# A mixture of experts whose first layer changes from twelve products a tile to Strassen's seven, in two long jobs an expert

## The chip, the cores and the metric

One core of a Trainium2 chip runs the whole program: attention and, behind and beside it, a mixture of experts. The metric is the device time of one execution in microseconds; a comparison is of medians over executions. Engines are named as in the profile: PE (TensorE, matmuls), PEld (its weight loads), DVE (VectorE), ACT (ScalarE), POOL (GpSimd, which also issues the indirect transfers) and SP (SyncE, which issues the plain ones). Each engine takes its instructions in the order in which the program holds them.

## The reference

`q`, `k`, `v` are 8 batches x 8 heads x 576 places x 64. Four heads attend to the 32 places before, four to places of the same remainder by 32. The result, 4608 rows of 512, goes through a mixture of eight experts, two of them for each row:

```python
logits = x @ w_gate
noisy_logits = logits + np.log1p(np.exp(x @ w_noise)) * noise
top2 = np.argpartition(-noisy_logits, 2, axis=1)[:, :2]
# top2_w: softmax over the two
for e in range(8):
    for k in range(2):
        mask = top2[:, k] == e
        h = np.maximum(x[mask] @ w1[e], 0.0)          # 512 -> 1024
        out[mask] += top2_w[mask, k, None] * (h @ w2[e])   # 1024 -> 512
```

All is float32. Which rows an expert gets is known only on the chip.

## The kernel before, in words

Attention runs first, with the gate and, for each expert, a list in memory of the rows (tokens) that chose it and their weights. An expert's list has 1216 places here: nine blocks of 128, and a half block of 64 that is empty for some experts.

**Matmuls of three products.** A float32 operand is split in a high and a low part of the type that TensorE takes at full rate; a product is hi x hi + lo x hi + hi x lo, three matmuls. The high part is a cast by ACT, the low part a subtraction by DVE: of the weights in `weights_of` (L905, L906), of the gathered rows in `transposes` (L1029, L1031), of the hidden layer in `layer1` (L1080, L1085).

**Jobs.** A job is an expert and a stretch of its list, (start, blocks, tail, batches that must be done). Before, experts 3 to 7 have four jobs each: three blocks from place 256, two from 640, two and the half block from 896, two from 0. Experts 0 to 2 have some of theirs early, beside attention. For each job the loop at the end of `experts` puts down: the gather of the next job's rows (POOL, four transfers a block, L982, into `xg`, two deep), layer 1, the loads and splits of the next expert's weights, the next job's transposes (DVE, L1022) and splits, and layer 2.

**Layer 1** (`layer1`, L1060) has eight tiles of 128 hidden features; each is one PSUM bank with 4 x 3 matmuls of the job's width, 256 or 384 columns, or 320 with a tail. In a job with a tail the ten inner matmuls run at 320, 288 or 256 columns by a value read on the chip. ACT's Relu gives the high part from the bank, DVE the low part.

**Layer 2** (`layer2`, L1114) has a bank a block: 24 matmuls of 512 columns; for the half block 16, or one of zeros (L1123) where it is empty. ACT scales the bank by the rows' weights into `prev` (L1138; for a half block DVE adds the second half, L1142), and POOL scatters `prev` to the result rows with an adding transfer (L1147).

**The order.** All this is put down as `Piece`s (engine, cost, what they read, write and allocate). `issue_all` walks them like a simulation: of the pieces whose predecessors are placed it places next, for each engine, the one that by its costs could start first, by rank where several could within 120 ns. A cost is 60 + 0.84 ns a column for ACT, 75 + 1.04 for DVE; a PSUM bank is handed to the piece that asks, free since longest first. `Ring` is a tile name with its depth: the k-th next allocation waits for the users of the one k before. POOL's transfers get a wait on the DVE or ACT instruction that the planner put ahead of them. So the costs and the rings, not the text, fix the order on each engine.

## Time and profile before

| | us |
|---|---|
| median of 3 executions | 1124.09 |
| lowest, highest | 1120.41, 1124.75 |
| the profiled execution, its own time | 1126.48 |
| its span in the trace | 1124.7 |
| mean granted clock of TensorE | 0.979 |

The page sums busy time of each engine over the span, shows it in 40 slices, and follows the chain of work that ended last back from the end. Rows of the chain and of the timeline give the start, the length and what ran; rows of groups give the busy sum, the mean in ns and the idle time before. Busy time of PE is a union of overlapping matmuls, so the length of one matmul row is longer than the distance to the next.

### The profile page before, as it was taken

To read this page: it belongs to the slowest core of one execution; us is meant where nothing else is said; L and a number is where in the kernel's file an instruction comes from. 1 tells how busy PE (TensorE), PEld (TensorE's weight loads), DVE (VectorE), ACT (ScalarE), POOL (GpSimd) and SP (SyncE) were. 2 spreads that over 40 slices of the span, in tenths; PEclk is the share of its full clock that TensorE was granted. 3 is DMA by queue.
4 is the path that set the end of the run, shared out by engine and by line. 5 is a ranking of instruction groups with operands and counts; after the bars stand their busy time and mean duration, and the time that the engine had idled before them with its cause. 6 is when DMAs were issued, how large, how long until landed. Compare 5 with 4: busy or idle time off the path is not lost.

```text
span 1124.7 us, 23405 instructions
## 1 busy us (share of the span) xinstructions
PE 1076.4 (96%) x8729; PEld 949.0 (84%) x8729; DVE 551.6 (49%) x1532; ACT 483.9 (43%) x1205; POOL 530.5 (47%) x654
## 2 busy tenths in 40 slices
PE   9888898998999999999999999999999999999994
PEld 7667677887889988998899989898989898898993
...
GB/s 187 183 167 212 209 168 202 203 191 215 231 78 156 114 49 44 125 119 120 123 130 131 46 63 184 54 46 81 167 46 48 109 130 43 56 149 54 43 33 22
DMA packets 167946, 133.01 MB, mean 118 GB/s; under 512 B 51636, under 2 KB 136116, under 8 KB 167812
## 3 DMA queue, kind: packets, MB, share of 16 engines
...
q14 instruction: 52, 0.43, 0.1%
HBM read 92.84 MB, written 39.39 MB: 118 GB/s over the span
## 4 chain that ended last, share of the span: by engine, by line
PE 86%; DVE 4%; issue 3%; ACT 3%; DMA 2%; another core or an unknown queue 1%; POOL 0%; POOLq 0%; DVEq 0%; ACTq 0%
PE bankH L1114 5%; PE bankD L1114 5%; PE bankE L1060 5%; PE bankB L1060 5%; PE bankA L1060 5%; PE bankC L1060 5%; PE bankH L1060 4%; PE bankB L1114 4%; PE bankF L1060 4%; PE bankG L1060 4%; PE bankD L1060 4%; PE bankA L1114 4%; PE bankF L1114 4%; PE bankC L1114 4%; PE bankE L1114 4%; PE bankG L1114 4%
## 5 line engine op out<-in xcount | busy, mean ns | idle before, releaser
L982 POOL DMA_INDIRECT xg<-x_dram,gxx x240 | 245.8, 1024 | 183.0 <-DVE xr L1022 80.7
L1147 POOL DMA_INDIRECT out_dram<-prev,tabt x80 | 135.3, 1691 | 104.2 <-ACT prev L1138 64.8
L833 POOL DMA_INDIRECT tab<-ent,addr x96 | 93.2, 971 | 106.6 <-issue 27.3
L1022 DVE STREAM_TRANSPOSE xr<-xg 128x512 f32<-128x512 f32 (+1 forms) x64 | 66.5, 1039 | 42.4 <-DMA xg<-x_dram,gxx 33.1
L1029 ACT CAST xhi<-xr 128x512 fp32r<-128x512 f32 (+1 forms) x64 | 37.8, 591 | 61.2 <-DVE xr L1022 58.9
L906 DVE TENSOR_TENSOR w2lo<-wraw,w2hi 128x512 fp32r<-128x512 f32 x80 | 52.2, 684 | 13.5 <-ACT w2hi L905 7.5
L906 DVE TENSOR_TENSOR w1lo<-wraw,w1hi 128x512 fp32r<-128x512 f32 x80 | 54.6, 686 | 2.8 <-issue 0.4
L1031 DVE TENSOR_TENSOR xlo<-xr,xhi 128x512 fp32r<-128x512 f32 (+1 forms) x64 | 42.2, 659 | 27.2 <-ACT xhi L1029 25.7
L905 ACT CAST w1hi<-wraw 128x512 fp32r<-128x512 f32 x80 | 49.0, 616 | 3.4 <-issue 3.3
L905 ACT CAST w2hi<-wraw 128x512 fp32r<-128x512 f32 x80 | 46.7, 618 | 7.4 <-DMA wraw<-in_moe_w_dram 6.4
L821 POOL COPY ent<-wt 96x12 f32<-96x12 f32 x8 | 1.6, 201 | 93.2 <-DVE wt L815 82.8
L1085 DVE SCALAR_TENSOR_TENSOR hlo<-bankE,hhi 128x256 fp32r<-128x256 f32 (+1 forms) x33 | 15.2, 460 | 58.1 <-ACT hhi L1080 39.8
L1060 PE MATMUL bankB<-xhi,w1hi 128*128 128x256 f32 (+3 forms) x136 | 40.8, 300 | 0.0
L1060 PE MATMUL bankE<-xhi,w1hi 128*128 128x256 f32 (+3 forms) x132 | 40.5, 307 | 0.0
L1060 PE MATMUL bankB<-xhi,w1lo 128*128 128x256 f32 (+3 forms) x136 | 40.3, 296 | 0.0
L1060 PE MATMUL bankB<-xlo,w1hi 128*128 128x256 f32 (+3 forms) x136 | 40.2, 295 | 0.0
L1060 PE MATMUL bankE<-xhi,w1lo 128*128 128x256 f32 (+3 forms) x132 | 40.0, 303 | 0.0
L1060 PE MATMUL bankE<-xlo,w1hi 128*128 128x256 f32 (+3 forms) x132 | 39.8, 302 | 0.0
L1060 PE MATMUL bankA<-xhi,w1hi 128*128 128x256 f32 (+3 forms) x128 | 38.9, 304 | 0.0
L1085 DVE SCALAR_TENSOR_TENSOR hlo<-bankD,hhi 128x256 fp32r<-128x256 f32 (+1 forms) x31 | 14.2, 458 | 50.0 <-ACT hhi L1080 40.0
L1060 PE MATMUL bankH<-xhi,w1hi 128*128 128x256 f32 (+3 forms) x128 | 38.6, 302 | 0.0
L1060 PE MATMUL bankC<-xhi,w1hi 128*128 128x256 f32 (+3 forms) x128 | 38.4, 300 | 0.0
...
## 6 DMA issues: line engine op xcount, KB each, us to landing
...
```

What stands on the lines that cost most here:

```text
L821: nc.gpsimd.tensor_copy(s["ent"].t[:, :, :, 1].bitcast(F32), s["wt"].t)
L833: st = nc.gpsimd.indirect_dma_start(out=tab, out_offset=bass.IndirectOffsetOnAxis(ap=s["addr"].t[:, t, kk:kk + 1], axis=0), in_=s["ent"].t ...
L905: Piece("ACT", act(512) + 30, lambda o: nc.scalar.copy(hi.t, raw.t), rank, read=[raw], alloc=[hi], expert=True)
L906: Piece("DVE", dve(512), lambda o: nc.vector.tensor_tensor(lo.t, raw.t, hi.t.bitcast(F32), ALU.subtract), rank, read=[raw, hi], alloc=[lo] ...
L982: dma(lambda o, g=g: nc.gpsimd.indirect_dma_start(out=xg.t[:, g, :], out_offset=None, in_=x_dram[:4 * known, :], in_offset=bass.IndirectOf ...
L1022: Piece("DVE", 8 * rows, lambda o, xg=xg, xr=xr, ng=ng, rows=rows: nc.vector.transpose(xr.t.rearrange("p (c x) -> p c x", c=ND)[:, :, :row ...
L1029: Piece("ACT", act(4 * rows), lambda o, view=view, cols=cols: nc.scalar.copy(xh.t[:, :, cols], view()), rank, read=[xr], expert=True, **{h ...
L1031: Piece("DVE", dve(4 * rows), lambda o, view=view, cols=cols: nc.vector.tensor_tensor(xl.t[:, :, cols], view(), xh.t[:, :, cols].bitcast(F ...
L1060: nc.tensor.matmul(ps.t[:, :width], a.t[:, 128 * d:128 * d + 128], c.t[:, d, :width], start=(m == 0), stop=(m == len(todo) - 1))
L1085: nc.vector.scalar_tensor_tensor(dst, ps.t[:, c0:c1], 0.0, hh.t[:, c0:c1].bitcast(F32), op0=ALU.max, op1=ALU.subtract)
L1114: nc.tensor.matmul(ps.t, HT[n, f][p[0]].t[:, cols], W2[n][f][p[1]].t, start=(m == 0), stop=(m == len(todo) - 1))
L1147: st = nc.gpsimd.indirect_dma_start(out=out[:known, :], out_offset=bass.IndirectOffsetOnAxis(ap=tb.t[:rows, i, 0:1], axis=0), in_=pv.t[:ro ...
```

## The change

Experts 3 to 7 get two jobs each, four blocks and the half from place 640 (576 places) and five blocks from 0 (640 places); the last part of expert 1 becomes one job of 576. Layer 1 of these eleven jobs is computed by Strassen's scheme with 7 products in Winograd's form: the rows are cut into two halves of 288 or 320 columns, the 512 inputs into two halves of 256, the 1024 features into pairs of tiles (i, i + 4). For each of four pairs `pair` makes seven products of 2 x 3 matmuls. They use seven combinations of weights (three quarters of `wraw` as loaded, and four sums in `Sa` and `Sb`, made by four adds of 256 columns on POOL) and seven of inputs (`XR` as transposed, and four sums `TS` on DVE), each split in hi and lo. Three banks a pair (a, b, f) take the products; ACT copies the first to `CC` (two deep), DVE combines the others with `CC`, ACT and DVE make the hi and lo parts `hp`. `ends` copies the half block's columns to a spare place. The half block's 64 places are always computed in layer 1. Layer 2 reads `hp` and has the same matmuls.

The new tiles take the place in SBUF of old ones: a `GATE` piece closes a pool when its last users are placed and opens the new one in its place. `prev` has three tiles instead of four. In the last job, the result rows of the job's places are gathered ahead (`previous`, POOL), DVE adds bank times weight to them, and the scatter writes without adding. A setting of the program's indirect transfers, `dynamic_dma_scratch_size`, becomes 8192.

```diff
-        [(0, 2, 0, 4), (256, 3, 0, 5), (640, 2, 0, B), (896, 2, 64, B)],
+        [(0, 2, 0, 4), (256, 3, 0, 5), (640, 4, 64, B)],
         [(0, 3, 0, 7), (384, 2, 0, 7), (640, 2, 0, 7), (896, 2, 64, B)],
-    ] + [[(0, 2, 0, B), (256, 3, 0, B), (640, 2, 0, B), (896, 2, 64, B)]] * (E - EARLY)
+    ] + [[(0, 5, 0, B), (640, 4, 64, B)]] * (E - EARLY)
     WID = 384
+    FAST = 4
+    HALF = 320
...
+    def swap(old, new, users, side):
+        def change(o):
+            if old:
+                spaces[old].close()
+            open_pool(new, side)
+        gates_at[new] = Piece("GATE", 0, change, 0, after=users)
...
-            ("prev", [128, DM], F32, 4)):
+            ("tabt", [128, 5, 3], I32, 3), ("gix", [128, 5], I32, 3), ("tabx", [128, 20, 3], I32, 2),
+            ("gxx", [128, 5, 4], I32, 2), ("xg", [128, 4, 128], F32, 2), ("prev", [128, DM], F32, 3)):
         R[name] = ring(ffn, shape, dtype, name, depth)
-    for layer in (1, 2):
-        for part in ("hi", "lo"):
-            R[f"w{layer}{part}"] = ring(wring, [128, 512], F32R, f"w{layer}{part}", NF)
+    for name, shape, dtype, depth in (
+            ("xr", [128, ND * 128], F32, 1), ("xhi", [128, ND, WID], F32R, 1), ("xlo", [128, ND, WID], F32R, 1),
+            ("w1hi", [128, 512], F32R, NF), ("w1lo", [128, 512], F32R, NF)):
+        R[name] = ring(pools["wplain"], shape, dtype, name, depth)
+    for name in ("hhi", "hlo"):
+        R[name] = ring(pools["hplain"], [128, WID], F32R, name, NF)
+    for part in ("hi", "lo"):
+        R[f"w2{part}"] = ring(wring, [128, 512], F32R, f"w2{part}", NF)
+    NPR = NF // 2
+    for where, name, shape, dtype, depth in (
+            ("xfast", "XR", [128, ND, 2 * HALF], F32, 1), ("xfast", "TS", [128, 4, HALF], F32, 1),
+            ("xfast", "xBhi", [128, 3, 2, HALF], F32R, 1), ("xfast", "xBlo", [128, 3, 2, HALF], F32R, 1),
+            ("xfast", "xThi", [128, 4, 2, HALF], F32R, 1), ("xfast", "xTlo", [128, 4, 2, HALF], F32R, 1),
+            ("xfast", "Sa", [128, 2, 256], F32, 1), ("xfast", "Sb", [128, 2, 256], F32, 1),
+            ("xfast", "CC", [128, 3 * HALF], F32, 2),
+            ("wfast", "fhi", [128, 7, 256], F32R, NPR), ("wfast", "flo", [128, 7, 256], F32R, NPR),
+            ("hfast", "hp", [128, 2, 4 * HALF], F32R, NPR)):
...
+        def add(dst, x, y):
+            nc.gpsimd.tensor_tensor(dst, x, y, ALU.add)
+        def first(o):
+            add(sa.t[:, 0, :], rb.t[:, :256], rb.t[:, 256:])
+            add(sa.t[:, 1, :], sa.t[:, 0, :], ra.t[:, :256])
+        def second(o):
+            add(sb.t[:, 0, :], ra.t[:, :256], rb.t[:, :256])
+            add(sb.t[:, 1, :], ra.t[:, 256:], sa.t[:, 1, :])
+        Piece("POOL", 1300, first, rank, read=[ra, rb], alloc=[sa], expert=True)
+        Piece("POOL", 1300, second, rank, read=[ra, rb, sa], alloc=[sb], expert=True)
...
+        parts = ((ra, lambda: ra.t.rearrange("p (a x) -> p a x", a=2), 0, 2), (rb, lambda: rb.t[:, None, 256:], 2, 3),
+                 (sa, lambda: sa.t, 3, 5), (sb, lambda: sb.t, 5, 7))
+        for src, view, a, b in parts:
...
+            split(bh, bl, lambda t: t[:, 0, :, :w], lambda: xr.t[:, :2, :w], [xr], "alloc", 2 * w)
+            for kk in range(2):
+                ts = R["TS"].new()
+                def sums(o, kk=kk, ts=ts):
+                    b11, b12 = xr.t[:, kk, :w], xr.t[:, kk, w:2 * w]
+                    b21, b22 = xr.t[:, 2 + kk, :w], xr.t[:, 2 + kk, w:2 * w]
+                    t = [ts.t[:, i, :w] for i in range(4)]
+                    nc.vector.tensor_tensor(t[0], b11, b12, ALU.subtract)
+                    nc.vector.tensor_tensor(t[1], t[0], b22, ALU.add)
+                    nc.vector.tensor_tensor(t[2], b12, b22, ALU.subtract)
+                    nc.vector.tensor_tensor(t[3], b21, t[1], ALU.subtract)
...
+            product(a, 0, bh, bl, 0, True, False, psum=[a, b, f])
+            x = step("ACT", act(w) + 30, lambda o: nc.scalar.copy(c21(), bank(a)()), read=[a], alloc=[cc])
+            product(b, 4, th, tl, 1, True, False, write=[b])
+            u2 = step("DVE", dve(w), tt(c12, c21, bank(b), ALU.subtract), read=[b, cc], write=[cc])
+            product(f, 3, th, tl, 0, True, False, write=[f])
+            w_ = step("DVE", dve(w), tt(c22, c21, bank(f), ALU.add), read=[f, cc], write=[cc])
+            product(a, 1, bh, bl, 1, False, True, write=[a], after=[x])
+            step("ACT", act(w) + 30, lambda o: nc.scalar.activation(hp.t[:, 0, :w], bank(a)(), AF.Relu), read=[a], alloc=[hp])
+            product(b, 5, th, tl, 2, False, False, write=[b], after=[u2])
+            v = step("DVE", dve(w), tt(c22, bank(b), c22, ALU.subtract), read=[b, cc], write=[cc])
+            def low(dst, src, hi):
+                nc.vector.scalar_tensor_tensor(dst, src, 0.0, hi.bitcast(F32), op0=ALU.max, op1=ALU.subtract)
+            product(f, 6, bh, bl, 2, False, True, write=[f], after=[w_])
+            step("DVE", dve(w), tt(c12, c12, bank(f), ALU.add), read=[f, cc], write=[cc])
+            step("DVE", dve(w), lambda o: low(hp.t[:, 1, :w], bank(a)(), hp.t[:, 0, :w]), read=[a, hp], write=[hp])
+            product(b, 2, th, tl, 3, False, True, write=[b], after=[v])
+            step("DVE", dve(w), tt(c21, bank(b), c21, ALU.subtract), read=[b, cc], write=[cc])
+            step("ACT", act(3 * w) + 30, lambda o: nc.scalar.activation(hp.t[:, 0, w:4 * w], cc.t[:, :3 * w], AF.Relu),
+                 read=[cc], write=[hp])
+            step("DVE", dve(3 * w), lambda o: low(hp.t[:, 1, w:4 * w], cc.t[:, :3 * w], hp.t[:, 0, w:4 * w]), read=[cc, hp],
+                 write=[hp])
+            if jobs[n][1][2]:
+                def ends(o):
+                    spare = hp.t[:, :, 4 * HALF - 128:].rearrange("p s (a g x) -> p a s g x", a=2, g=2)
+                    for part in range(2):
+                        nc.scalar.copy(spare[:, part], hp.t[:, part, :4 * w].rearrange(
+                            "p (s g x) -> p s g x", s=2, g=2)[:, :, :, w - 32:].bitcast(F32))
+                step("ACT", 2 * act(128), ends, read=[hp], write=[hp])
...
+        def previous(n, i, rank, others):
+            gi = G_[n][1]
+            if n + 1 < NJOB:
+                return None
+            pv = R["prev"].new()
+            dma(lambda o: nc.gpsimd.indirect_dma_start(
+                out=pv.t, out_offset=None, in_=out,
+                in_offset=bass.IndirectOffsetOnAxis(ap=gi.t[:, i:i + 1], axis=0)),
+                128 * 2048, rank, eng="POOL", read=[gi], alloc=[pv], after=others + zero, expert=True)
+            return pv
...
+            if kept:
+                Piece("DVE", dve(512), lambda o: nc.vector.scalar_tensor_tensor(
+                    pv.t, ps.t, tb.t[:, i, 1:2].bitcast(F32), pv.t, op0=ALU.mult, op1=ALU.add), rank, expert=True,
+                      read=[ps, tb, pv], write=[pv])
...
-                    **({} if first else {"compute_op": ALU.add}))
+                    **({} if first or kept else {"compute_op": ALU.add}))
...
+            if turned:
+                swap("wplain", "wfast", users_of("w1hi", "w1lo", "xhi", "xlo", "xr") + [gates_at["xfast"]], "right")
```

Three places of the instruction order, as they stand in the programs (the operation, the tile written and those read, its shape, and on what it waits: an engine's name is that engine, DMAHW and DMASW a transfer).

On PE, the start of a job of 384 columns of an expert, before:

```order
L1060 MATMUL bankC<-xhi,w1hi 128x384 [waits Activation_49]
L1060 MATMUL bankC<-xlo,w1hi 128x384 [waits DVE_49]
L1060 MATMUL bankC<-xhi,w1lo 128x384
L1060 MATMUL bankC<-xhi,w1hi 128x384
...
L1060 MATMUL bankD<-xhi,w1hi 128x384
L1060 MATMUL bankD<-xlo,w1hi 128x384
```

and of the change, in the first two pairs of a job of 640 places:

```order
L1188 MATMUL bankF<-xBhi,fhi 128x320
...
L1188 MATMUL bankD<-xBhi,fhi 128x320 [waits Activation_49]
...
L1188 MATMUL bankC<-xThi,fhi 128x320
...
L1188 MATMUL bankE<-xThi,fhi 128x320
...
L1188 MATMUL bankG<-xThi,fhi 128x320 [waits Activation_49]
...
L1188 MATMUL bankF<-xBhi,fhi 128x320 [waits Activation_49]
...
L1188 MATMUL bankC<-xThi,fhi 128x320 [waits DVE_49]
...
L1188 MATMUL bankE<-xBhi,fhi 128x320 [waits DVE_49]
```

Before, a job goes on from bank to bank without a wait once its inputs are there; now two pairs stand interleaved, and a bank is used again within the pair after ACT or DVE has read it.

On DVE, between the bank readers of a job of 384 before:

```order
L1085 SCALAR_TENSOR_TENSOR hlo<-bankC,hhi 128x384 [waits Activation_49]
L906 TENSOR_TENSOR w2lo<-wraw,w2hi 128x512 [waits DMAHW2_49,Activation_49]
L906 TENSOR_TENSOR w2lo<-wraw,w2hi 128x512 [waits DMAHW3_49,Activation_49]
L1085 SCALAR_TENSOR_TENSOR hlo<-bankD,hhi 128x384 [waits Activation_49]
L906 TENSOR_TENSOR w2lo<-wraw,w2hi 128x512 [waits DMAHW4_49,Activation_49]
L1085 SCALAR_TENSOR_TENSOR hlo<-bankF,hhi 128x384 [waits Activation_49]
```

and of the change, in a job of 640 places:

```order
L1196 TENSOR_TENSOR CC<-bankG,CC 128x320 [waits PE_49]
L989 TENSOR_TENSOR flo<-wraw,fhi 128x512 [waits DMAHW4_49,Activation_49]
L989 TENSOR_TENSOR flo<-wraw,fhi 128x256 [waits DMAHW5_49,Activation_49]
L1212 SCALAR_TENSOR_TENSOR hp<-CC,hp 128x960 [waits Activation_49] x2
L1196 TENSOR_TENSOR CC<-CC,bankB 128x320 [waits PE_49,Activation_49]
L989 TENSOR_TENSOR flo<-Sa,fhi 128x512 [waits Pool_49]
L1196 TENSOR_TENSOR CC<-CC,bankD 128x320 [waits PE_49]
L989 TENSOR_TENSOR flo<-Sb,fhi 128x512 [waits Pool_49]
```

The next expert's weight low parts, some of which wait for POOL's sums, now stand between combinations that PE waits for.

On DVE, behind the last low parts of expert 0, before:

```order
L1085 SCALAR_TENSOR_TENSOR hhi<-bankG,hhi 128x64
L1031 TENSOR_TENSOR xlo<-xr,xhi 128x4x128 [waits Activation_49]
L906 TENSOR_TENSOR w1lo<-wraw,w1hi 128x512 [waits DMAHW3_49,PE_49,Activation_49]
L1022 STREAM_TRANSPOSE xr<-xg 128x4x4x32 [waits DMASW3_49,DMASW2_49,DMASW5_49,DMASW0_49,DVE_49]
L1031 TENSOR_TENSOR xlo<-xr,xhi 128x4x128 [waits Activation_49]
```

and the end of what stands there ahead of the first new products' inputs:

```order
L1149 TENSOR_TENSOR xTlo<-TS,xThi 128x4x288 [waits Activation_49]
L989 TENSOR_TENSOR flo<-Sa,fhi 128x512 [waits Pool_49]
L1159 TENSOR_TENSOR TS<-XR 128x288 [waits DVE_49]
L1160 TENSOR_TENSOR TS<-TS,XR 128x288 [waits DVE_49]
L1161 TENSOR_TENSOR TS<-XR 128x288
L1162 TENSOR_TENSOR TS<-XR,TS 128x288 [waits DVE_49]
L1362 SCALAR_TENSOR_TENSOR prev<-bankC,tabt,prev 64x512 [waits Activation_49]
L989 TENSOR_TENSOR flo<-Sb,fhi 128x512 [waits Pool_49]
L989 TENSOR_TENSOR flo<-wraw,fhi 128x256 [waits DMAHW0_49,Activation_49]
L1149 TENSOR_TENSOR xTlo<-TS,xThi 128x4x288 [waits Activation_49]
```

Before, weight low parts of the next expert were made one by one among the low parts of this one; now they, the sums and the splits all stand behind.

178 lines of the change are left out of this document (144 added, 34 removed).

## The prediction, made before the changed kernel ran

> **What bounds the kernel now.** I read the page's engine shares and slices first, then the chain of waits, then a table of windows over the part of the program that the change touches. Columns of a window: its length, then busy time and count of PE, PE's weight loads, DVE, ACT and POOL, the granted clock, DMA share and GB/s.
>
> ```profile
> span 1124.7 us, 23405 instructions
> PE 1076.4 (96%) x8729; PEld 949.0 (84%) x8729; DVE 551.6 (49%) x1532; ACT 483.9 (43%) x1205; POOL 530.5 (47%) x654
> PE 86%; DVE 4%; issue 3%; ACT 3%; DMA 2%; another core or an unknown queue 1%; POOL 0%; POOLq 0%; DVEq 0%; ACTq 0%
> 541.60:587.10 45.50, 45.50 (x290) 40.93 (x289) 26.47 (x52) 20.91 (x43) 29.13 (x27) 1.00 0.55 138
> 587.10:693.50 106.40, 106.40 (x618) 95.85 (x618) 46.71 (x83) 37.17 (x74) 65.06 (x61) 1.00 0.43 91
> 1008.30:1109.80 101.50, 101.48 (x602) 91.12 (x600) 29.74 (x58) 25.69 (x52) 41.09 (x38) 1.00 0.28 46
> sum 568.20, PE 568.18 PEld 511.58 DVE 232.52 ACT 186.31 POOL 310.48; mean PE 94.70 PEld 85.26 DVE 38.75 ACT 31.05 POOL 51.75
> ```
>
> TensorE bounds it: from 541.6 us to its last matmul it is busy 568.18 of 568.20 us at full clock. DVE is used 41% there, ACT 33%, POOL 55%. So TensorE time that is removed comes off the end one for one, until an engine that feeds or empties it can't follow. TensorE's instructions, banks included, stand in the same order before and after up to the first new product, which takes the place of the job at 541.6 us. I forecast nothing for the part ahead of it.
>
> **The work removed.** Durations are the pitch from one group of matmuls to the next in the chain of waits (start, us, what), since single matmul rows overlap.
>
> ```profile
> 434.04 1.40 PE bankA L1060 x12
> 564.38 1.46 PE bankE L1060 x12
> 643.32 1.63 PE bankE L1060 x12
> 456.44 1.76 PE bankC L1060 x12
> 693.68 2.08 PE bankC L1060 x12
> 576.07 5.59 PE bankE L1114 x24
> ```
>
> Twelve matmuls of 256 columns take 1.40 us, 116.7 ns each; of 320 columns 1.76, 146.6 ns; of 384 columns 2.08, 173.3 ns. The 1.63 row is a tail block's f-tile, ten of 288 and two of 320: (1.63 - 2 x 0.1466)/10 = 133.4 ns for 288. The 1.46 row is one whose half block is empty (ten of 256, two of 320). A later full block of layer 2 has 24 of 233 ns; it stays.
>
> Before, layer 1 from 541.6 us on: five jobs of 384 at 8 x 2.08 = 16.64 us, eleven of 256 at 8 x 1.40 = 11.2 us, six tails (two with 1.63 per f-tile, one with 1.76, three with 1.46: 75.2 us together with rounding). That is 83.2 + 123.2 + 75.2 = 281.6 us. After: six jobs of 576 places and five of 640, each with 4 pairs x 7 products x 6 matmuls = 168. 6 x 168 x 133.4 ns = 134.5 us, 5 x 168 x 146.6 ns = 123.1 us, 257.6 in all. **-24.0 us** if TensorE stays full.
>
> **What the new products need of DVE.** Each pair now asks DVE for five combinations of a bank with CC, one low part from a bank and one of three quarters; each job for five transposes, two groups of four sums and four splits; each expert for sixteen weight low parts, 28 pieces of 256 columns where there were eight of 512.
>
> ```profile
> 596.73 3.08 DVE L906 TENSOR_TENSOR w2lo<-wraw,w2hi 128x512 fp32r<-128x512 f32 x5
> 599.84 0.56 DVE L1085 SCALAR_TENSOR_TENSOR hlo<-bankA,hhi 128x384 fp32r<-128x384 f32 x1
> 600.32 0.55 DVE L1085 SCALAR_TENSOR_TENSOR hlo<-bankB,hhi 128x384 fp32r<-128x384 f32 x1
> 575.58 0.42 DVE L1085 SCALAR_TENSOR_TENSOR hlo<-bankB,hhi 128x256 fp32r<-128x256 f32 x1
> 575.91 0.21 DVE L1085 SCALAR_TENSOR_TENSOR hhi<-bankB,hhi 128x64 fp32r<-128x64 f32 x1
> 536.35 1.10 DVE L1022 STREAM_TRANSPOSE xr<-xg 128x512 f32<-128x512 f32 x1
> ```
>
> Back to back these advance 0.33 us at 256 columns, 0.48 at 384, 0.62 at 512 from start to start (596.73 to 599.84 holds five); 0.60 without the step to another kind. That is close to 0.07 us plus 1.035 ns a column, for two SBUF inputs (L906) and for bank with SBUF (L1085) alike, so I price the combinations, which the trace does not have, by it: 0.37 for 288, 0.40 for 320, 1.06 for 960.
>
> The order of DVE's instructions tells what stands between a job's first and last combination. Job of 640 places: four pairs at 5 x 0.40 + 0.40 + 1.06 = 3.46 are 13.8 us; a transpose and a half one 1.7; a group of sums 1.5; a split 0.7; nine weight low parts, seven of 512 and two of 256 columns, 7 x 0.60 + 2 x 0.33 = 4.9. Together 22.6 us against 168 x 0.1466 = 24.6 us of TensorE, 92%. The job of 576 counts 18.4 against 22.4 us. Below 100% this hides behind the products only if nothing is needed early. The tightest place that I find is the ring of two CC tiles: the third pair's copy into CC waits for the first pair's last low part. From the job's start: products until the first pair's last one 11.4 us, then 0.4 and 1.0 (that pair's last combination and ACT's three quarters), 1.06 (its low part), 0.94 and 0.6 (other work that stands ahead in DVE's queue), 0.44 (the copy; ACT's 384 columns took 0.49): 15.85 us, when TensorE is at its nineteenth product, 15.8 us, and next wants what this copy frees. There is no slack. Bounds: 0, should low parts of weights be done early, and 5 us an expert, which is about ten combinations late by the 0.5 us of one more instruction ahead. I take **+1.5 us for each of five experts, +7.5**, near the row that says 92%, and +1 for the first new job.
>
> **The entrance.** The new weights and inputs lie where the old ones lay, so their writes wait for the last old reader.
>
> ```profile
> 529.10 1.46 PE bankG L1060 x12
> 530.56 5.59 PE bankA L1114 x24
> 536.16 5.60 PE bankB L1114 x24
> 541.76 0.23 PE bankC L1123
> ```
>
> Expert 0's last layer 1 ends at 530.5; its last low parts are off DVE at about 531.4. From there TensorE has two full blocks of layer 2 and an empty half block to do, until 541.9. In DVE's new order there stand, behind those low parts and ahead of the last xTlo, which the second product reads: eight weight low parts of 512 columns and four of 256 (6.1 us), a transpose and a half one (1.7), eight sums (3.0), splits of 576 and three times 1152 columns (0.67 + 3 x 1.26 = 4.5), a half block's row sum (0.75): 16 us, so 547.4. TensorE does one product first (0.8 us), to 542.7. **+5.** Bounds: 3, if DVE runs a sixth faster than these rows, and 10, if ACT's casts, which come ahead of each low part, set the pace; a stall of this length may cost clock too (the window behind the last matmul, below, was granted 0.92). Late next is only the first pair's CC work, behind products.
>
> **POOL and DMA.** The w1 transfers keep their number and size, row gathers and scatters too (nine blocks and a half an expert), and tables are loaded for two jobs, not four. New on POOL are sixteen adds of 256 columns an expert, with two inputs, of which the trace has none.
>
> ```profile
> L126 POOL TENSOR_SCALAR_AFFINE_SELECT mask_l<-mask_l 64x192 bf16<-64x192 bf16 x1 | 0.4, 352 | 0.1
> L118 POOL TENSOR_SCALAR_AFFINE_SELECT mask_s<-mask_s 64x72 bf16<-64x72 bf16 x2 | 0.5, 240 | 1.3 <-DVE mask_s L117 1.3
> 562.05 0.97 POOL L982 DMA_INDIRECT xg<-x_dram,gxx  x1 [0.30 <-issue]
> ```
>
> One input costs 112 ns for 120 columns more, 0.93 ns each: 0.41 us at 256 columns. I bound the two-input add by that and by twice it, 0.8, and take 0.6 as the middle: 9.6 us an expert, on an engine that is busy 65 of 106 us (a gather counts 1.27 with its gap, so some 80 of 106 with gaps). They run for the next expert's weights, beside layer 2 and products of this one, so I add nothing; without that cover the next weights would come later by up to two pairs' adds, 5 us an expert. [...]
>
> **The end.** The last job reads its old result rows ahead, adds on DVE and writes plainly.
>
> ```profile
> 1109.87 0.69 ACT L1138 ACTIVATE prev<-bankB,tabt 128x512 f32<-128x512 f32 x1 [4.96 <-PEq L1228]
> 1110.83 1.56 POOL L1147 DMA_INDIRECT out_dram<-prev,tabt  x1 [4.10 <-ACT prev L1138]
> L1147 POOL DMA_INDIRECT out_dram<-prev,tabt x80: 1002/1630/4372, 202.4 to 1110.8; - x80
> 1110.00:1115.00 5.00, 0.00 (x0) 0.00 (x0) 0.00 (x0) 0.56 (x1) 1.56 (x1) 0.92 0.42 57
> 1115.00:1120.00 5.00, 0.00 (x0) 0.00 (x0) 0.00 (x0) 0.00 (x0) 0.00 (x0) 0.50 0.00 0
> ```
>
> DVE's multiply-add takes the place of ACT's 0.69 us (0.60 by the rows above, or 0.75 at a half block); the scatter's issue 1.0 (the shortest of L1147; the first lists are written plainly) instead of 1.56; its bytes land within the window to 1115. **-1**, bounds -2 and 0. The five gathers, 1.3 us each on POOL, wait for expert 6's scatters and lie beside the last 50 us, where POOL is idle most of the time. The ring of prev falls from four tiles to three: blocks come every 5.6 us, scatters take 1.6 and land within a few us, so two are in flight. Cover gone, a block would wait some 2 us.
>
> **The sum.** Profiled execution 1126.48 us (span 1124.7), 0.2% above the median of 1124.09. 1126.5 - 24.0 + 7.5 + 1 + 5 - 1 = 1115.0; less the same 2.4 us 1112.6, told as **1112 us**.
>
> **The rivals.**
> *A: TensorE stays full.* For it: 92% and 82% are below one, and two pairs are interleaved over six banks. Against: the CC chain without slack, the entrance. Entrance 3, the rest 0: 1124.1 - 24 + 3 - 1 = 1102, and 1101 with the end at -2.
>
> *B: late gathers hold the combinations.* DVE waited for gathered rows at transposes:
>
> ```profile
> DVE xr L1022 <- DMA xg<-x_dram,gxx: 20.2, 7, 9.0
> ```
>
> That is 20.2 us in 7 waits since 541 us, the longest 9.0, for which TensorE did not wait, as eight banks lay between. Now combinations are queued behind a transpose. TensorE's order lets it go on for five products (5 x 0.88 = 4.4 us) before it wants a bank back that DVE has just been given, and for two (1.7 us) where DVE already lags, as 92% lets expect. If the waits stay, with the latter: 20.2 - 7 x 1.7 = 8.3 us, 1112 + 8.3 = 1120; with the former only the longest shows, 9.0 - 4.4 = 4.6. For it: POOL has more to do between gathers. Against: transposes can now be spread over fewer, longer jobs.
>
> *C: slower, the adds hold DVE.* If a POOL add and a DVE operation with two SBUF inputs exclude each other, every add that falls into a window makes DVE longer by its own length. In the order half of an expert's adds (8) stand in the job of 640. DVE has 22.6 + 8 x 0.7 = 28.2 us for 24.6 there, 3.6 lost beside the 1.5: 5 x 5.1 = 25.5 instead of 7.5, so 1112 + 18 = 1130; with adds of 0.8 us 5 x 4.4 = 22 more, 1134. It passes the time of before at adds of 0.54 us: 22.6 + 4.3 - 24.6 = 2.3 an expert, 11.6 in all. For it: DVE's sums, splits and weight low parts have two SBUF inputs, and POOL's computing beside such work was on a few columns only. Against: most of the 13.8 us of pair work reads a bank and one SBUF input, and beside POOL's gathers the low parts did not stretch, their mean being that of an undisturbed one (0.68):
>
> ```profile
> L906 DVE TENSOR_TENSOR w1lo<-wraw,w1hi 128x512 fp32r<-128x512 f32 x80 | 54.6, 686 | 2.8 <-issue 0.4
> ```
>
> [...]
>
> *D: the change does not act as said*, some wide stretch runs as before: 1124. Nothing in the order speaks for it.
>
> **How the numbers follow.** Forecast 0.51 (its own range 1105 to 1118), A 0.17, B 0.17, C 0.13, D 0.02. About 0.5%, 5.6 us, is what a measurement of this kernel can tell from no change: faster is below 1118.5, slower above 1129.7. Faster: nearly all of the forecast, A and a bit of B, 0.69. Slower: most of C and a tail of B, 0.12. Within: 0.19. The range that leaves out no more than 2 in 10 is 1099 to 1126: it holds A, less half of the runs' spread of 4 us, the forecast and B, and ends ahead of C.
>
> **What would show it.** Right: windows of products at 22 to 24 us a job with DVE at eight or nine tenths and TensorE idle in pieces below a microsecond, put down to DVE's combinations; one gap of some 5 us at about 543; pitches of 133 and 147 ns. Wrong: gaps behind a transposing DVE that waits for a gather (B), DVE operations with two SBUF inputs that become longer while POOL adds (C), pitches that differ, or a gap at the entrance above 10 us.

## The result: 2.8% slower

| | median, us | range | executions |
|---|---|---|---|
| before | 1124.42 | 1120.41 to 1126.42 | 4 |
| changed | 1155.53 | 1150.49 to 1161.38 | 4 |

The ratio is 1.0283, with a 95% interval of 1.0221 to 1.0345: 31 us slower where I had forecast 12 us faster. The page of the changed kernel and the groups that are new in it:

```profile
span 1156.7 us, 22949 instructions
PE 1072.4 (93%) x8465; PEld 934.2 (81%) x8465; DVE 725.5 (63%) x1746; ACT 531.1 (46%) x1241; POOL 636.9 (55%) x733
PE 70%; DVE 13%; issue 6%; POOL 3%; DMA 3%; ACT 3%; another core or an unknown queue 1%; POOLq 0%; DVEq 0%; ACTq 0%
L972 POOL TENSOR_TENSOR Sa<-wraw 128x256 f32<-128x256 f32 x24 | 28.8, 1201 | 24.2 <-DVE flo L989 23.6
L1149 DVE TENSOR_TENSOR xTlo<-TS,xThi 128x1152 fp32r<-128x1152 f32 (+1 forms) x22 | 36.6, 1663 | 1.3 <-ACT xThi L1147 1.3
```

264 matmuls fewer, yet PE's share falls to 93%, and its part of the chain from 86% to 70%. Most of what it lost there went to DVE; POOL, which had none of the chain, has 3%.

**Where the time went.** Cut at the end of the last plain layer 1 (530.56 us before; 528.16 now, where the chain below leaves L1253) and at the start of the last matmul:

```profile
1148.67 0.39 PE L1330 MATMUL bankD<-w2hi,hp 128*128 128x512 f32 x1
```

Before, that matmul started at 1109.38:

```profile
1109.38 0.40 PE L1114 MATMUL bankB<-w2hi,hlo 128*128 128x512 f32 x1
```

Ahead of the first cut: -2.4 us. Between: 578.8 before, 620.5 now, +41.7. Behind: 15.3 before, 8.0 now, -7.3. The sum is the +32.0 of the two spans. By the products alone the middle part should have fallen by 24.0, so the stalls in it are worth 65.7 us, where I had put 13.5.

Windows of seven of the eleven new jobs (the first four and the last three), each with the layer 2 that follows (columns as in the prediction):

```profile
539.00:601.50 62.50, 50.40 (x267) 43.91 (x265) 50.61 (x82) 31.25 (x59) 52.22 (x48) 0.89 0.43 109
601.50:664.20 62.70, 53.32 (x282) 47.42 (x282) 42.55 (x63) 24.55 (x44) 46.64 (x45) 0.92 0.47 102
664.20:722.00 57.80, 53.77 (x289) 46.98 (x288) 45.09 (x66) 24.50 (x40) 47.28 (x45) 1.00 0.38 81
722.00:775.50 53.50, 50.51 (x281) 44.71 (x280) 33.23 (x51) 18.66 (x34) 42.75 (x40) 0.97 0.44 96
990.40:1050.10 59.70, 55.47 (x290) 48.54 (x290) 40.79 (x63) 24.36 (x41) 40.78 (x39) 0.97 0.38 82
1050.10:1096.10 46.00, 45.18 (x267) 40.13 (x265) 28.56 (x50) 18.09 (x33) 13.89 (x11) 1.00 0.31 50
1096.10:1148.60 52.50, 52.50 (x289) 47.06 (x289) 19.44 (x33) 8.52 (x14) 11.92 (x11) 1.00 0.18 49
```

The first two jobs leave PE idle for 12.1 and 9.4 us, at clocks of 0.89 and 0.92; the seven after them 1.8 to 4.2 us each. The last two jobs, in which no weights of a next expert are summed any more, leave 0.8 and 0.0 us. That, and the place of the worst loss, pointed at the weight sums. What PE waited for from 540 us on was mostly the copies of ACT (16.2 us by the names in the trace) and the combinations of DVE (14.7 us), and no wait names the weights `fhi` or `flo` themselves (one of 1.9 us, at the first product, names a sum of POOL). The two largest entries (total us, times, the longest):

```profile
PE bankG L1188 <- DVE CC L1196: 8.4, 5, 2.5
PE bankC L1188 <- ACT CC L1201: 5.8, 1, 5.8
```

**The chain at the entrance** (start, us, what):

```profile
526.65 1.51 PE bankG L1253 x12
...
542.23 1.94 DVE xBlo L1149 x2
544.17 1.27 DVE xTlo L1149
545.44 0.61 DVE flo L989
...
547.17 1.64 POOL out_dram L1367
548.81 2.42 POOL Sa L972
551.23 0.05 issue
551.27 0.03 POOLq L1367
551.31 0.73 POOL Sa L972
552.04 0.02 issue
552.06 0.63 ACT fhi L987
```

I had DVE's stream end at 547.4 and PE go on from there. It ended about 3 us later (its last split is the 549.30 row below), and the chain did not go back to PE: DVE's low part of the first `Sa` frees the only tile for the second pair's sums (545.44), POOL has a gather and a scatter ahead of them, the first sum lasts 2.4 us, and ACT's cast waits for it. On ACT stands behind that cast what PE wants:

```profile
549.30 1.35 DVE L1149 TENSOR_TENSOR xTlo<-TS,xThi 128x1152 fp32r<-128x1152 f32 x1
552.06 0.62 ACT L987 CAST fhi<-Sa 128x512 fp32r<-128x512 f32 x1 [3.22 <-POOL Sa L972]
552.59 0.40 ACT L1207 ACTIVATE hp<-bankD 128x288 fp32r<-128x288 f32 x1
552.89 0.39 ACT L1201 COPY CC<-bankH 128x288 f32<-128x288 f32 x1
553.33 0.61 PE L1188 MATMUL bankH<-xBhi,fhi 128*128 128x288 f32 x1 [4.33 <-ACT CC L1201]
555.17 0.44 PE L1188 MATMUL bankF<-xTlo,fhi 128*128 128x288 f32 x1
```

The copy of bank H stood behind the cast of a weight that comes later, and PE stood still for 4.33 us until it was made. I had looked for the queue on DVE only. The last row shows one more thing that I had misread: in this job PE makes both products of bank D and both of bank H first, so the first product that reads `xTlo` is the fifth, not the second, and by then the splits had been ready for some 4 us.

**Sums and low parts side by side.** Rows of POOL, then of DVE:

```profile
603.02 1.28 POOL L972 TENSOR_TENSOR Sa<-wraw 128x256 f32<-128x256 f32 x1
604.38 1.74 POOL L972 TENSOR_TENSOR Sa<-Sa,wraw 128x256 f32<-128x256 f32 x1
685.43 0.92 POOL L972 TENSOR_TENSOR Sb<-wraw 128x256 f32<-128x256 f32 x1
686.32 0.73 POOL L972 TENSOR_TENSOR Sb<-wraw,Sa 128x256 f32<-128x256 f32 x1
```

```profile
597.55 1.34 DVE L1149 TENSOR_TENSOR xTlo<-TS,xThi 128x1152 fp32r<-128x1152 f32 x1
602.62 2.90 DVE L1149 TENSOR_TENSOR xTlo<-TS,xThi 128x1152 fp32r<-128x1152 f32 x1
686.08 0.47 DVE L1196 TENSOR_TENSOR CC<-bankC,CC 128x320 f32<-128x320 f32 x1
686.48 1.12 DVE L989 TENSOR_TENSOR flo<-Sa,fhi 128x512 fp32r<-128x512 f32 x1
```

A split of 1152 columns, 1.34 us alone, lasts 2.90 beside two sums, and these 1.28 and 1.74 instead of 0.73. A low part of 512 columns takes 1.12 instead of 0.68. The combination at 686.08, whose second input is a bank, keeps its 0.47 beside a sum. Spans of POOL are rough in these profiles, so DVE's rows carry the reading.

**The clock after a stall.** The windows around one stall in the middle of a job:

```profile
732.00:735.50 3.50, 1.50 (x10) 1.04 (x8) 1.26 (x4) 0.00 (x0) 1.89 (x2) 1.00 0.51 140
735.50:739.50 4.00, 3.52 (x15) 3.52 (x16) 2.83 (x6) 2.04 (x3) 2.70 (x3) 0.57 0.12 33
739.50:744.00 4.50, 4.50 (x37) 4.50 (x36) 4.50 (x8) 1.91 (x6) 3.86 (x7) 1.00 0.16 40
```

PE stood still for about 2.2 us; for the next 3 us it was granted 0.57, and a product of 288 columns went on at 0.24 us a matmul instead of 0.133: twelve of them took 3.0 us instead of 1.6. This stall of 2.2 us thus cost some 3.6. From the clocks of the jobs' windows (0.11 x 62.5 + 0.08 x 62.7 us, 0.03 of five of the other nine jobs' 50 to 60 us) I estimate that the lower clock cost some 20 of the 65.7 us. That fits the rest of the account: PE's idle time in the eleven windows is 42.8 us, which leaves 22.9 for slower matmuls.

### The profile page after: what moved, and what is told of

Read it like the earlier page. It is cut to its first block, busy times and chain, and to the rows that moved or that the text cites. A ratio compares the mean times of both kernels' runs of the same rounds, so it can differ in the third digit from the quotient of the medians.

```text
span 1156.7 us, 22949 instructions
## 1 busy us (share of the span) xinstructions
PE 1072.4 (93%) x8465; PEld 934.2 (81%) x8465; DVE 725.5 (63%) x1746; ACT 531.1 (46%) x1241; POOL 636.9 (55%) x733
## 4 chain that ended last, share of the span: by engine, by line
PE 70%; DVE 13%; issue 6%; POOL 3%; DMA 3%; ACT 3%; another core or an unknown queue 1%; POOLq 0%; DVEq 0%; ACTq 0%
PE bankG L1330 6%; PE bankH L1330 5%; PE bankD L1330 4%; PE bankA L1330 4%; PE bankC L1330 4%; DVE flo L989 3%; PE bankE L1188 3%; PE bankF L1330 3%; PE bankG L1188 2%; PE bankB L1330 2%; PE bankF L1188 2%; DVE CC L1196 2%; PE bankD L1188 2%; PE bankB L1253 2%; PE bankB L1188 2%
## 5 line engine op out<-in xcount | busy, mean ns | idle before, releaser
L1141 DVE STREAM_TRANSPOSE XR<-xg 128x512 f32<-128x512 f32 (+1 forms) x55 | 57.3, 1049 | 62.8 <-DMA xg<-x_dram,gxx 54.0
L1218 ACT ACTIVATE hp<-CC 128x864 fp32r<-128x864 f32 (+1 forms) x44 | 41.9, 961 | 57.1 <-DVE CC L1196 56.1
L1330 PE MATMUL bankG<-w2hi,hp 128*128 128x512 f32 x176 | 58.7, 395 | 0.0
L1212 DVE SCALAR_TENSOR_TENSOR hp<-CC,hp 128x864 fp32r<-128x864 f32 (+1 forms) x44 | 50.6, 1164 | 3.4 <-ACT hp L1218 2.9
L1330 PE MATMUL bankA<-w2hi,hp 128*128 128x512 f32 x144 | 47.6, 396 | 0.0
L1330 PE MATMUL bankD<-w2hi,hp 128*128 128x512 f32 x128 | 41.9, 395 | 0.0
L1149 DVE TENSOR_TENSOR xTlo<-TS,xThi 128x1152 fp32r<-128x1152 f32 (+1 forms) x22 | 36.6, 1663 | 1.3 <-ACT xThi L1147 1.3
L1330 PE MATMUL bankF<-w2hi,hp 128*128 128x512 f32 x112 | 36.8, 395 | 0.0
L1330 PE MATMUL bankG<-w2lo,hp 128*128 128x512 f32 x88 | 34.8, 395 | 0.0
L1330 PE MATMUL bankC<-w2hi,hp 128*128 128x512 f32 x104 | 34.7, 396 | 0.0
```

Source lines behind the costliest of these rows:

```text
L1141: nc.vector.transpose(dst, xg.t[:, :ng, :].rearrange("p g (i c) -> p g c i", c=ND))
L1149: Piece("DVE", dve(n_), lambda o: nc.vector.tensor_tensor(dst(lo.t), src(), dst(hi.t).bitcast(F32), ALU.subtract), rank, read=[*srcs, hi], ...
L1212: nc.vector.scalar_tensor_tensor(dst, src, 0.0, hi.bitcast(F32), op0=ALU.max, op1=ALU.subtract)
L1218: step("ACT", act(3 * w) + 30, lambda o: nc.scalar.activation(hp.t[:, 0, w:4 * w], cc.t[:, :3 * w], AF.Relu), read=[cc], write=[hp])
L1330: nc.tensor.matmul(ps.t, stationary(f, p[0]), W2[n][f][p[1]].t, start=(m == 0), stop=(m == len(todo) - 1))
```

## The experiments

They ran on several chips. On some the kernel before takes 1088 to 1092 us, on others 1120 to 1125, and the change costs 1.1% on the first kind and 2 to 2.8% on the second. So each run is told as its ratio to the kernel before on its own chip, and the five groups, each on one chip, are kept apart.

### First group (before: 1089.95)

**The change without its sums.** The factors that should be sums of weights are the weights as loaded:

```diff
-        Piece("POOL", 1300, first, rank, read=[ra, rb], alloc=[sa], expert=True)
-        Piece("POOL", 1300, second, rank, read=[ra, rb, sa], alloc=[sb], expert=True)
-                 (sa, lambda: sa.t, 3, 5), (sb, lambda: sb.t, 5, 7))
+                 (ra, lambda: ra.t.rearrange("p (a x) -> p a x", a=2), 3, 5),
+                 (rb, lambda: rb.t.rearrange("p (a x) -> p a x", a=2), 5, 7))
```

> The changed kernel without POOL's sixteen weight sums an expert: ACT and DVE split weights as loaded in their place, so their work stays in number and width, and the result is wrong in the first layer. Theory 1 (the sums cost: a sum lasts 1.1 to 1.2 us instead of 0.6, it and DVE's operations with two SBUF inputs hold each other up, and ACT's casts and DVE's low parts that wait for a sum stand ahead of bank readers): the first two new jobs lose some 10 us instead of 32, jobs of 640 places lose 1 instead of 2 to 7, in all about 30 us less, 1125. Theory 2 (gathered rows come late and hold the combinations): within 5 us of the changed kernel, 1150 or more, and the jobs of 576 keep their gaps of 2.5 us. Theory 3 (DVE simply has too much work): nearly no gain, since DVE's own instructions stay.

0.9849 (0.9794 to 0.9904): 1073 us, 2.6% or 28 us below the change's ratio on a chip of the same kind (1.0109, next group). The theory of the sums holds. Windows of its four first new jobs, the first two in the first two rows:

```profile
503.60:541.00 37.40, 32.02 (x196) 29.86 (x196) 35.67 (x64) 24.64 (x51) 26.65 (x22) 0.91 0.52 141
541.00:610.10 69.10, 66.12 (x353) 56.53 (x352) 47.49 (x78) 26.65 (x45) 56.09 (x48) 1.00 0.51 109
610.10:663.00 52.90, 52.90 (x290) 47.23 (x289) 37.94 (x65) 23.77 (x40) 31.54 (x27) 1.00 0.42 91
663.00:711.00 48.00, 48.00 (x281) 42.91 (x280) 30.15 (x50) 18.98 (x34) 30.98 (x29) 1.00 0.44 94
```

Idle is 5.4 and 3.0 us at the entrance; the third and fourth job are full to the hundredth. DVE has the same instructions as in the change, so their number alone (the forecast's 92%) does not stall PE on this kind of chip.

**Rows that nobody waits for.** Among DVE's waits in the changed kernel from 540 us on, by what it waited for (total us, times, the longest), this is the first:

```profile
DVE XR L1141 <- DMA xg<-x_dram,gxx: 45.8, 12, 9.0
```

In this run the transposes read a tile of weights in place of the gathered rows, so layer 1 of the new jobs works on other numbers:

```diff
-                    nc.vector.transpose(dst, xg.t[:, :ng, :]...
-                Piece("DVE", 8 * rows, turned, rank, read=[xg]
+                    nc.vector.transpose(dst, still.t.bitcast(F32)...
+                Piece("DVE", 8 * rows, turned, rank, read=[still]
```

> The changed kernel with DVE's transposes for the new jobs reading a tile of weights that lies ready, not the gathered rows: the gathers still run, nobody waits for them, the result is wrong. Theory 2 (late rows): the gaps of 2.4 to 2.7 us in the jobs of 576, with the lower clock behind each, go; 15 to 20 us less, about 1137. Theory 1 (the sums): 3 us at most, the first two jobs and the jobs of 640 stay as they are.

1.0068 (1.0038 to 1.0097), where the change itself has 1.0109 on a chip of the same kind (next group): some 4 us, with intervals that leave 0 to 11, not 15 to 20. The gaps behind late rows in the first trace were real; freeing the rows gave back little of them, and what held PE up in their place was not followed up.

**The sums on DVE:**

```diff
-            nc.gpsimd.tensor_tensor(dst, x, y, ALU.add)
+            nc.vector.tensor_tensor(dst, x, y, ALU.add)
-        Piece("POOL", 1300, first, rank, read=[ra, rb], alloc=[sa], expert=True)
-        Piece("POOL", 1300, second, rank, read=[ra, rb, sa], alloc=[sb], expert=True)
+        Piece("DVE", 2 * dve(256), first, rank, read=[ra, rb], alloc=[sa], expert=True)
+        Piece("DVE", 2 * dve(256), second, rank, read=[ra, rb, sa], alloc=[sb], expert=True)
```

> The changed kernel with the sixteen weight sums an expert on DVE instead of POOL, 0.33 us each by the rows of before, 5.3 us an expert more on DVE; the result is right. Theory 1 (length of a POOL sum, mutual hold and its chain): 10 to 20 us less than the changed kernel, about 1140. Theory 3 (DVE's load binds): slower than the changed kernel by up to 5 x 5 us, 1160 to 1180.

0.9988 (0.9960 to 1.0016): 1.2% below the change's 1.0109, though DVE has sixteen operations an expert more to do (means of 0.41 to 0.43 us). The theory that DVE's load binds falls.

**Result rows late again, in the changed kernel.** `previous` never gathers, so the last job's blocks are scattered with an addition, as all others are:

```diff
-            if n + 1 < NJOB:
-                return None
+            return None
```

> The changed kernel without the early gather of result rows in the last job: ACT scales, the scatter adds, as before. From the last matmul to the end the changed kernel's trace takes 7.3 us, that of before 14.9. If that is the early gather's doing, this run is 7 us slower, 1162; by my forecast of 1 us, 1156.5; if it is the ring or the setting of the transfers, no difference.

1.0178 (1.0125 to 1.0232), 0.7% or 7.5 us above the change's ratio in the next group, with intervals that leave 0 to 15. In the traces of these two the span ends 12.7 and 8.1 us after the start of the last matmul, so 4.6 us of it lie in the tail. The early gather is worth some 5 us or more, not 1.

### Second group (before: 1092.27)

**The change itself** on this kind of chip, with no edit.

> The changed kernel itself, on the chip and in the company of the next three, so that they have something to be compared with: the four runs so far were on a chip where the kernel before takes 1090 us. By the first chip's ratio it takes 1121; by the run with the late result rows (1108) less 7 us, 1101.

1.0109 (1.0059 to 1.0159), 1104 us: between the two guesses, nearer to the second.

**Sums that only write.** Each sum becomes two fills with a constant, so those factors are not the weights' sums:

```diff
-            nc.gpsimd.tensor_tensor(dst, x, y, ALU.add)
+            nc.gpsimd.memset(dst, 0.01)
+            return nc.gpsimd.memset(dst, 0.01)
```

> The changed kernel with each of POOL's sums replaced by two fills of the same 256 columns: POOL is busy about as long (two times 0.3 us against 0.73 for a sum that nothing holds up), and ACT and DVE still wait for it, but it reads nothing; the result is wrong. If the mutual hold of POOL's reads and DVE's second input is the price, DVE's low parts of 512 columns come back from 0.9 to 0.68 us and nearly the whole gain of the kernel without sums is there, some 25 us. If POOL's length and the chain behind it are the price, at most a third of that.

1.0025 (1.0006 to 1.0043), 9 us below the change beside it. DVE's groups (busy us, mean ns | idle before) of the change, and then of this run:

```profile
L989 DVE TENSOR_TENSOR flo<-Sa,fhi 128x512 fp32r<-128x512 f32 x23 | 21.9, 953 | 7.7 <-ACT fhi L987 7.7
L1149 DVE TENSOR_TENSOR xTlo<-TS,xThi 128x1152 fp32r<-128x1152 f32 x12 | 20.2, 1684 | 0.0
```

```profile
L990 DVE TENSOR_TENSOR flo<-Sa,fhi 128x512 fp32r<-128x512 f32 x23 | 15.8, 686 | 4.9 <-ACT fhi L988 4.9
L1150 DVE TENSOR_TENSOR xTlo<-TS,xThi 128x1152 fp32r<-128x1152 f32 x12 | 16.2, 1349 | 0.0
L972 POOL MEMSET Sa<- 128x256 f32 x46 | 17.4, 377 | 26.5 <-DVE flo L990 26.5
L973 POOL MEMSET Sa<- 128x256 f32 x46 | 14.4, 312 | 2.6
```

With POOL writing only, DVE's operations are back at what they take alone, 0.686 and 1.349 us. So it is POOL's reading that held them. The combinations with a bank take the same in both runs: those of bank E with 288 and 320 columns have means of 0.443 and 0.480 us in the change, 0.442 and 0.482 here. This hold is about a third of what the sums cost: 0.8% of before (the intervals leave 0.3 to 1.4), against 2.6% between the change and the kernel without sums (on two chips of one kind). The rest is left with a POOL that is busy two times 0.34 us for a sum and reads nothing. By elimination it lies in POOL's length and in what waits for it; no run separates these two, and leaving out the sums also lets the planner order the other work anew. These fills don't wait for the weights to arrive as a sum does, so the two thirds are a lower bound.

**The kernel before with the early rows alone**: `previous`, the multiply-add and the plain write, in its last job:

```diff
-        def layer2(n, i, rank, others):
+        def previous(n, i, rank, others):
+            gi = G_[n][1]
+            if n + 1 < NJOB:
+                return None
+            pv = R["prev"].new()
+            dma(lambda o: nc.gpsimd.indirect_dma_start(
+                out=pv.t, out_offset=None, in_=out,
+                in_offset=bass.IndirectOffsetOnAxis(ap=gi.t[:, i:i + 1], axis=0)),
+                128 * 2048, rank, eng="POOL", read=[gi], alloc=[pv], after=others + zero, expert=True)
+            return pv
+
+        def layer2(n, i, rank, others, pv):
...
+            if kept:
+                Piece("DVE", dve(512), lambda o: nc.vector.scalar_tensor_tensor(
+                    pv.t, ps.t, tb.t[:, i, 1:2].bitcast(F32), pv.t, op0=ALU.mult, op1=ALU.add), rank, expert=True,
+                      read=[ps, tb, pv], write=[pv])
...
-                    **({} if first else {"compute_op": ALU.add}))
+                    **({} if first or kept else {"compute_op": ALU.add}))
```

> The kernel before, with only the early gather of result rows in the last job (two blocks), DVE's multiply-add and a plain scatter. By the two tails, 14.9 and 7.3 us, 7 us faster than before; by my forecast 1 us, that is no difference.

0.9911 (0.9879 to 0.9942). Its last matmul starts at 1072.16 and its span ends at 1079.6, 7.4 us later. POOL's last rows here, and the last one of the changed kernel with late rows:

```profile
1073.27 1.03 POOL L1165 DMA_INDIRECT out_dram<-prev,tabt  x1 [7.36 <-issue]
1074.61 0.99 POOL L1165 DMA_INDIRECT out_dram<-prev,tabt  x1 [0.30 <-issue]
```

```profile
1090.89 1.56 POOL L1366 DMA_INDIRECT out_dram<-prev,tabt  x1 [4.04 <-ACT prev L1357]
```

That one's span ends at 1102.1: 9.7 us after the issue of an adding scatter ends (1092.45), against 4.0 us after a plain one (1075.60). The other traces agree: the kernel before, on the slower kind of chip, ends 12.3 us after its last adding issue, and all runs with a plain last scatter 4.0 to 5.3 us after it.

**Sums on DVE, and expert 1's last part plain**, the sums as in the first group, and:

```diff
-        [(0, 2, 0, 4), (256, 3, 0, 5), (640, 4, 64, B)],
+        [(0, 2, 0, 4), (256, 3, 0, 5), (640, 2, 0, B), (896, 2, 64, B)],
```

> The sums on DVE, and expert 1's last part as before in two plain jobs, so that expert 3's first job is the first new one. The products of that half job save only 22.9 - 22.4 = 0.5 us. If the entrance costs by the work that DVE has behind it, it comes again at expert 3 with the same 8 to 10 us, but the second job's 5 to 10 us go: 5 to 10 us faster than the sums on DVE alone, 1080 to 1085 where before is 1090. If the second job's loss comes from the entrance's lateness, no difference.

0.9916 (0.9888 to 0.9945), 0.7% below the sums on DVE alone. The half job cost more than the 0.5 us that it saves: here the first new job leaves PE idle for 7.6 us, where the first two of the sums on DVE alone leave 12.5.

### Third group (before: 1124.87, the slower kind of chip)

**A planner that knows the sums' price:**

```diff
-        Piece("POOL", 1300, first, rank, read=[ra, rb], alloc=[sa], expert=True)
-        Piece("POOL", 1300, second, rank, read=[ra, rb, sa], alloc=[sb], expert=True)
+        Piece("POOL", 2300, first, rank, read=[ra, rb], alloc=[sa], expert=True)
+        Piece("POOL", 2300, second, rank, read=[ra, rb, sa], alloc=[sb], expert=True)
```

> The changed kernel with the planner's price of a pair of POOL sums raised from 1300 to 2300 ns, what the trace shows (two of 1.1 to 1.2 us); nothing else, the result is right. If the sums hurt because the order was planned with too short a price, so that casts and low parts stand ahead of bank readers before their sum is there, this gains 10 to 15 us: 1090 to 1095 where the changed kernel is 1104 and before 1092. If the length of the sums and their hold on DVE are the price wherever they stand, it gains less than 4 us.

1.0225 (1.0131 to 1.0319), against the change's 1.0283 and 1.0200 on chips of this kind: no gain is seen, though intervals of 1% don't rule 10 us out. PE's idle time in the nine later jobs is 22 us here and 21 in both of the other traces, and in the first two 15.4 against 21.5 and 20. So a wrong price of the sums in the planner is at most a small part of the cause.

The next three start from sums on DVE and expert 1's last part plain (its own ratio on this kind of chip is in the next group: 1.0047).

**No pacing**: the wait that a POOL transfer of the experts gets on an instruction of DVE or ACT is left out.

```diff
-            if e == "POOL" and o.lat:
+            if e == "POOL" and o.lat and not o.expert:
```

> Sums on DVE, expert 1's last part plain, and POOL's transfers of the experts without the wait on a DVE or ACT instruction that the planner put ahead of them. If rows come late because of that wait, the remaining stalls behind transposes go: 3 to 6 us faster than 1083. If not, no difference, or slower where transfers now hinder those of weights.

1.0448 (1.0361 to 1.0536), 4% more than the same kernel with it (1.0047, next group). The expected gain is not there: the pacing serves. Behind the first new job PE is idle for 34 us in this trace, against 13 with the pacing; why unpaced transfers cost so much was not followed up.

**Inputs' splits first at the entrance**, the weights of pairs 2 and on behind them:

```diff
-            if change:
+            early = turned and change
+            if early:
+                for i in range(2):
+                    W[1, i] = weights_fast(jobs[n + 1][0], i, rank + 20)
+                transposes_fast(n + 1, rank + 3)
+                xdone = pieces[-1]
+                for i in range(2, NPR):
+                    W[1, i] = weights_fast(jobs[n + 1][0], i, rank + 20, [xdone])
+            if change and not early:
```

> Sums on DVE, expert 1's last part plain, and at the entrance the splits of the third and fourth pair's weights made to wait for the last split of the new inputs. By the order theory (DVE has 16 us of work ahead of the second product there, 4 to 5 of which the first pairs don't need), 4 to 6 us of the 9 lost there go: 1077 to 1079. If late rows set the entrance, 0 to 2 us.

1.0091 (1.0057 to 1.0124); no gain over 1.0047, and PE is idle for 11.6 us in the first new job, against 9.6. This order of the splits at the entrance does not shorten it.

**Three tiles of gathered rows:**

```diff
-            ("gxx", [128, 5, 4], I32, 2), ("xg", [128, 4, 128], F32, 2), ("prev", [128, DM], F32, 3)):
+            ("gxx", [128, 5, 4], I32, 2), ("xg", [128, 4, 128], F32, 3), ("prev", [128, DM], F32, 2)):
```

> Sums on DVE, expert 1's last part plain, with three tiles of gathered rows in place of two (and two of result rows in place of three, for space). If the depth of the row tiles makes rows late, 3 to 8 us faster than 1083; if result rows then wait for their scatters, up to 5 us slower; no difference if neither is tight.

1.0102 (0.9981 to 1.0224): not told apart from the rest. Its span ends 10.6 us after the start of the last matmul, against 8.0 with three tiles of result rows, as it would if result rows wait for their scatters.

### Fourth group (before: 1120.36, the slower kind)

**The change once more**, beside the runs of this group.

> The changed kernel once more, to be compared with the next three on one chip: a ratio of 1.028 to the kernel before on a chip where that takes 1124, 1.011 where it takes 1091.

1.0200 (1.0124 to 1.0276).

**The change without its sums**, with the first group's edit, on this kind of chip.

> No sums on POOL (the low and high parts stay; the result is wrong). If the sums are the cause on the slower chip too, 0.98 to 1.00 of before there, at least 25 us below the changed kernel; if late rows are the main cause there, only half the 31 us go, 1.013 of before or more. On the faster chip 0.985 again.

0.9988 (0.9954 to 1.0022): 2.1%, 22 us below the change beside it. The sums are the main cause on this kind of chip too, in about the size that they have on the other (2.6%), if a little less than the 25 us expected. The kind's own extra, 0.9 to 1.4%, is still there without them. So the jobs are not full here as they were on the faster kind: the third to the eleventh leave PE idle for 9.7 us together, against 1.5 there. The fourth job here, and the first of PE's waits from 648 us on:

```profile
701.30:753.70 52.40, 48.88 (x282) 43.24 (x281) 30.23 (x51) 18.79 (x34) 29.79 (x29) 1.00 0.42 86
PE bankG L1187 <- DVE CC L1195: 3.7, 3, 1.4
```

Of these 9.7 us, 6.2 are waits for DVE's combinations and 2.8 for ACT's copies.

**Neither sums nor waits for rows**, both edits of the first group together:

```diff
+                 (ra, lambda: ra.t.rearrange("p (a x) -> p a x", a=2), 3, 5),
+                 (rb, lambda: rb.t.rearrange("p (a x) -> p a x", a=2), 5, 7))
...
+                Piece("DVE", 8 * rows, turned, rank, read=[still], expert=True, **{"write" if i else "alloc": [xr]})
```

> No sums, and DVE's transposes of the new jobs read a ready tile (the result is wrong). If sums and late rows are together the whole loss but for the entrance, the time is that of before less 24 us of products, less 8 us at the end, plus 10 us at the entrance: 0.980 of before. If a loss of DVE's order is left, 0.99 or more.

1.0037 (1.0000 to 1.0074): not below the kernel without sums. Freeing the rows gains nothing here. Without the wait for rows the planner also orders things otherwise (in this run the third new job, from 640 us, loses most of what the first two gain), so this does not show what free rows are worth at best.

**Sums on DVE, expert 1's last part plain**, the second group's kernel on this kind of chip.

> Sums on DVE and expert 1's last part plain; the result is right. On the faster chip 0.992 of before. On the slower one, if that chip's extra loss comes through POOL's sums, the same 0.99; if it comes through late rows, 1.00 to 1.01.

1.0047 (1.0008 to 1.0087), 1.5% below the change beside it, but not below the kernel before.

### Fifth group (before: 1088.22)

**No sums, and expert 1's last part plain**, the edits of the first and the second group together.

> No sums on POOL, and expert 1's last part as two plain jobs (the result is wrong). If the half job of expert 1 carries the stalls at the entrance, its second half of them goes: 8 to 10 us less than without sums alone, 0.976 on the faster chips, 0.990 on the slower. If the entrance only moves to expert 3, no difference: 0.985 and 0.999.

0.9860 (0.9826 to 0.9894), the same as without sums alone (0.9849). PE is idle for 8.7 us in the first new job, where the first two of the kernel without sums leave 8.4. So the entrance moves to expert 3 and costs what it cost. That the work DVE has behind a tile's last reader sets this price is not shown. Without sums, then, the half job has no extra price; with the sums on DVE it had one.

**The kernel before with the early rows alone**, a second time.

> The kernel before with the early result rows alone (right): 0.991 of before on either chip, since its gain lies behind the last matmul, where no transfer of inputs is left; if the slower chip's memory matters there, between 0.985 and 0.995.

0.9929 (0.9904 to 0.9953). Of the versions that compute everything, this one, the kernel before with early result rows, is the fastest found: 0.7 to 0.9% below before, on two chips of the faster kind; on the slower kind it was not run. The one with sums on DVE and expert 1 plain is as good on the faster kind of chip and not on the slower.

## Why the prediction was wrong, by its own steps

- **Work removed, -24.0 us:** right in size. The pitches are those forecast (products of 288 and 320 columns run at 0.79 and 0.88 us for six), and without the sums whole jobs run without a gap on the faster kind of chip.
- **POOL, "so I add nothing": the step that failed.** I priced a sum at 0.6 us and bounded it at 0.8. It takes 0.73 alone and 1.1 to 1.2 in the means of its four groups. Worse, I set its cover by POOL's share of time (65 of 106 us) and not by what waits: `Sa` and `Sb` are single tiles, so sum, cast, low part and next sum follow each other, and behind each cast on ACT and each low part on DVE stand readers of banks. The sums cost 2.1% (22 us) on one chip beside the change, and about 2.6% on the other kind. The 5 us an expert that I gave for lost cover come near this size, but by another way: I meant weights that come late, and PE waited for banks.
- **Rival C** named the price that I left out. That a POOL add and a DVE operation with two inputs in SBUF exclude each other was supposed, and no row of before shows it; the changed kernel shows that DVE's operations become longer beside POOL's sums: 1.12 us for 0.68, 2.90 for 1.34. The rival gave 1130 to 1134, and even that was too little, as it counted the hold on DVE alone; the fills show that to be about a third.
- **+7.5 us in the windows from DVE's load and the two CC tiles:** without sums the third and fourth new jobs show 0.0 us idle on the faster kind of chip, and the nine later jobs 1.5 together, so nothing of the term is seen there. On the slower kind, on which I had forecast, they leave 9.7 us without sums, mostly in waits for DVE's combinations. That is near the term's size, but 6.1 us of it fall in jobs of 576, to which I had given slack, so the nearness is luck; whether the two CC tiles play a part is not shown. The change itself leaves 21.3 us in these nine jobs.
- **The entrance, +5 us:** in the kernel without sums PE's idle in the first two jobs is 8.4 us, with a clock of 0.91 for 37 us, about 12 together on the faster kind of chip, above my upper bound of 10; on the slower kind the idle time alone is 14.1 us. In the changed kernel it is 17.6 us on the faster kind and 21.5 on the slower, at a lower clock, as the second pair's sums came on top. I had PE wait for the last `xTlo` at its second product; it waited for ACT's copies, and read that tile first at its fifth. That the clock falls after a stall I had written as a possibility; it did (0.57 for some 3 us behind one of 2.2), and by my estimate (20 of 65.7 us) it is a third of the stalls' price.
- **The end, -1 us:** the sign was right, the size -7.3. I had priced the issue of the scatter and let its bytes land by 1115 either way; the span ends later after the issue of an adding scatter than after that of a plain one, by some 5 us on the faster kind of chip (9.7 against 4.0 to 5.1) and 7 on the slower (12.3 against 4.0 to 5.3). The trace of before had only adding scatters at its end, so it could not show the difference.
- **Rival B, late rows:** the waits came, but freeing them gave 4 us on one chip, and nothing on another where the sums were out as well. A wait that a trace names last need not be worth its length.
- What stays open: why the slower kind of chip loses another 1% or so with the change, with or without the sums. Its attention part is slower too (in the kernel without sums the last plain layer 1 ends at 524.2 us against 492.5), and transfers are what that part is full of (in the kernel before the DMA share is 0.67 up to 530.56 us and 0.40 from there to the last matmul), but no run took the memory apart.
